# Low parts of the last layer's prepared weights by ScalarE and an adding transfer in place of a VectorE subtraction

## The chip, the cores and the metric

The kernel runs on one core of one Trainium2 chip. The metric is the device time of one execution in microseconds (us). The engines are called as the profile calls them: PE (TensorE), DVE (VectorE), ACT (ScalarE), POOL (GpSimd) and SP (SyncE, which here only begins transfers).

## The reference, cut to what matters

```python
def reference(**kwargs):
    ...
    attn_out = _attn_ref(**attn_kwargs)            # q, k, v, s: 2 x 8 heads, 576 rows, 64 wide
    x = np.ascontiguousarray(attn_out.transpose(0, 2, 1, 3)).reshape(B * S, H * D)   # 1152 x 512
    x = _moe_ref(x=x, **moe_kwargs)                # 8 experts, 512 -> 1024 -> 512, all of them for every row
    return _moe2_ref(x=x, **moe2_kwargs)

def _moe2_ref(x, w_in, w_out):                     # the last layer: 512 -> 2048 -> 512
    h = x @ w_in
    g = np.maximum(h, 0.0) + np.log1p(np.exp(-np.abs(h)))
    return (g @ w_out).astype(np.float32)
```

`w_in` and `w_out` are drawn as 64-bit floats, and the host hands them over as raw 64-bit words.

## The kernel before, in words

After attention, the rows (1152 x 512) stay in SBUF and the kernel walks 20 blocks `x` of 512 hidden columns: 16 for the experts (`NX`), then 4 for the last layer (`NL`). Products are made in fp32r. Each fp32 operand is split in a high part (rounded to fp32r by an ACT copy) and a low part (the raw word less the high part, on DVE or POOL), and each product is three matmuls: high by high, high by low, low by high. A block's first product is a seven-product scheme on 2 x 2 sub-blocks (class `Unit`, `p1` to `p7`, two units `a` and `b`, tile `ph`), its second is `downs` (tile `py`, three matmuls each, two PSUM banks `y1` and `y2`; `total`, line 554 or 378, adds a finished bank to `acc` on DVE).

The order is written out by hand, and each engine takes its instructions in the order in which the program writes them. `play` walks strings of tokens: `a1` ... `b7` are products of six matmuls, `d` is one step of `downs`, tokens with `=` or `w` start the preparation of the next block's weights. A block of an expert is one `A_SEQ` (30 steps) and one `B_SEQ` (34 steps):

```python
A_SEQ = "a1 b1 a2 b2 =0 d d a6 d d b6 d d a7 d d b7 =1 d a5 d b5 d a3 d b3 d a4 d b4 d d"
B_SEQ = ("d d =2 a1 d d b1 d a2 d b2 d a6 d b6 d a7 d b7 d a5 d b5 d d w0 a3 d d w2 b3 d d w1 a4 d d w3 b4")
```

After each step, `step` (line 1244) runs one piece of each list of side work. From block 2 to block 13 it also advances the generator `conv`, made by `convert` (line 1082), by one piece at every second step; what `conv` has not done by block 14 is done at once there. `convert` prepares the weights of the last layer, in 16 jobs of 4 blocks each:

- `fetch` (line 1099, SP) loads 128 x 512 64-bit words into the tile `f`, two of them per job.
- `narrow` (lines 1104 to 1125, six pieces) makes fp32 of them: DVE lines 1108, 1110, 1112, 1115, 1118, 1119, 1121, ACT line 1109, and one addition on POOL, line 1124. The result stands in the tile `c8` (128 x 8 x 256, one buffer; the trace calls it `c`).
- POOL (line 1140) adds and subtracts blocks, which gives all eight blocks of `c8`.
- For four pairs `c` of these blocks, ACT writes the high part to `ch` (line 1148), DVE writes raw less high to `cl` (line 1150), and SP stores both to the DRAM tiles `wd` (line 1154). `ch` and `cl` have three buffers each; a piece ends after line 1148 and after line 1150.

A job has 22 pieces (2 x 6, 2, 4 x 2). `c8` has one buffer, so line 1109 of the next job, which writes into it, comes after the last read of the old one. On SP the loads of the experts' raw weights (line 141, tile `raw`) and the fetches stand in one queue with these stores. On POOL the same queue has the sums of the experts' first weights (lines 161 to 170) and half of the low parts of their second weights (line 220). ACT copies finished products out of PSUM (lines 468 and 427) in the same queue as lines 1109 and 1148; in a unit, the copy after `a5` must be done before `a3` writes the same bank.

Of the kernel before, what the change touches and what calls it, by code (L numbers as in the profile page):

```python
# [13 lines left out]
AF = mybir.ActivationFunctionType  # L14
ALU = mybir.AluOpType
# [5 lines left out]
def attention_moe_ffn(ctx, tc, q, k, v, s, w_gate, w1, w2, w_in, w_out, out):  # L21
    nc = tc.nc
# [11 lines left out]
    NX = w1.shape[0]  # L34
# [18 lines left out]
    def f(ap):  # L53
        return ap.bitcast(F32)
# [506 lines left out]
    with tc.manual_schedule():  # L561
        with ExitStack() as att:
# [64 lines left out]
            for j, queue, engine in ((0, nc.sync, nc.gpsimd), (1, nc.scalar, nc.vector)):  # L627
                queue.dma_start(out=s0[j * D:j * D + NR, :],
                                in_=s.rearrange("b (x two) s -> two (b x) s", two=2)[j].unsqueeze(1).to_broadcast([B * NP, 4, S]))
# [452 lines left out]
        def convert(cv):  # L1082
            CW = WQ // 2
            top = float(np.uint32(0x47EFFFFF).view(np.float32))
            low = float(np.uint32(0x38100000).view(np.float32))
            half = 2.0 ** -20
            jobs = []
            for x in range(NL):
                for p in range(2):
                    jobs.append((1, x, p, [w_in[2 * x + p][:, c * CW:(c + 1) * CW] for c in range(2)]))  # L1090
                for r in range(2):
                    jobs.append((2, x, r, [w_out[2 * x + i][:, r * CW:(r + 1) * CW] for i in range(2)]))
            todo = [z for *_, c in jobs for z in c]
            got = {}

            def fetch(i):
                if i < len(todo):
                    t = cv.tile([P, 2 * CW], U32, tag="f64", name="f64")
                    nc.sync.dma_start(out=t, in_=todo[i].bitcast(U32))
                    got[i] = t  # L1100

            def narrow(i, m):
                t64 = got.pop(i)
                r = t64.rearrange("p (f two) -> p f two", two=2)
                lo, hi = r[:, :, 0], r[:, :, 1]
                t = cv.tile([P, CW], U32, tag="ct", name="ct")
                hf = hi.bitcast(F32)
                nc.vector.tensor_scalar(hf, hf, -top, top, ALU.max, ALU.min)
                nc.scalar.activation(out=m, in_=hf, func=AF.Abs)
                nc.vector.tensor_scalar(t, hi, 5, 2, ALU.logical_shift_left, ALU.logical_shift_right)  # L1110
                yield
                nc.vector.scalar_tensor_tensor(out=t, in0=hi, scalar=0xC0000000, in1=t,
                                               op0=ALU.bitwise_and, op1=ALU.bitwise_or)
                yield
                nc.vector.scalar_tensor_tensor(out=m, in0=m, scalar=low, in1=f(t), op0=ALU.is_ge, op1=ALU.mult)
                yield

                nc.vector.tensor_scalar(t, m.bitcast(U32), 0xFF800000, None, ALU.bitwise_and)
                nc.vector.tensor_scalar(lo, lo, 9, 0x35800000, ALU.logical_shift_right, ALU.bitwise_or)
                yield  # L1120
                nc.vector.scalar_tensor_tensor(out=f(t), in0=lo.bitcast(F32), scalar=half, in1=f(t),  # L1121
                                               op0=ALU.subtract, op1=ALU.mult)
                yield
                nc.gpsimd.tensor_tensor(out=m, in0=m, in1=f(t), op=ALU.add)  # L1124
                fetch(i + 2)
                yield

            fetch(0)
            fetch(1)
            for _ in range(4):  # L1130
                yield
            for j, (which, x, n, _) in enumerate(jobs):
                t = cv.tile([P, 8, HW], F32, tag="c8", name="c8", bufs=1)
                for c in range(2):
                    yield from narrow(2 * j + c, t[:, 2 * c:2 * c + 2, :].rearrange("p b n -> p (b n)"))
                for o, a, b, op in (((4, 0, 3, ALU.add), (6, 1, 0, ALU.subtract), (7, 4, 1, ALU.subtract),
                                     (5, 2, 7, ALU.subtract)) if which == 1 else
                                    ((4, 1, 0, ALU.subtract), (6, 3, 1, ALU.subtract), (5, 3, 4, ALU.subtract),
                                     (7, 2, 5, ALU.subtract))):
                    nc.gpsimd.tensor_tensor(out=t[:, o], in0=t[:, a], in1=t[:, b], op=op)  # L1140
                    if o == 6:
                        yield
                yield
                for c in range(4):
                    o = int(which == 1 and c == 0)
                    u = slice(2 * c + o, 2 * c + 2)
                    h, l = (cv.tile([P, 2, HW], F32R, tag="c" + k, name="c" + k, bufs=3)[:, o:] for k in "hl")
                    nc.scalar.activation(out=h, in_=t[:, u], func=AF.Copy)
                    yield
                    nc.vector.tensor_tensor(out=l, in0=t[:, u], in1=f(h), op=ALU.subtract)  # L1150
                    yield
                    for k, y in enumerate((h, l)):
                        d = wd[1][x, n][:, k, u] if which == 1 else wd[2][x][:, k, u, n]
                        nc.sync.dma_start(out=d, in_=f(y))
# [86 lines left out]
        tick = [0, 0, 0, 0]  # L1241
        dense = [False]

        def step(z=""):

            tick[0] += 1
            tick[1] += 1
            tick[2] = 0 if z[1:] == "2" else tick[2] + 1
            if x < XE:
                if tick[1] >= (5 if tick[3] > 10 and tick[3] % 2 else 3) and tick[2] > 2 and not dense[0]:  # L1250
                    next(gates, None)
                    tick[1] = 0
                    tick[3] += 1
            elif x < NX - 2 and tick[0] % 2:
                next(conv, None)
            for todo in (back, side, bot):
                while todo and next(todo[0], 1):
                    todo.pop(0)
# [15 lines left out]
        def play(seq, todo, d=None):  # L1274


            for z in seq.split():
                if z[0] in "=w":
                    dense[0] = z[0] == "w"
                if z[0] == "=":  # L1280
                    back.append(prep1(x + 1, int(z[1])))
                    continue
                if z[0] in "tu":
                    side.append(turn(int(z[1]), z[0] == "t"))
                    continue
                if z[0] == "w":
                    back.append(prep2(x + 1, int(z[1])))
                    continue
                if z[0] in "xy":
                    bot.append(prep_b(x + 1, z[1:]) if z[0] == "x" else prep_t(x + 1, int(z[1])))  # L1290
                    continue
                if z[0] in "EF":
                    side.append(h_steps(x, int(z[1]), z[0]))
                    continue
                if z[0] == "X":
                    bot.append(prep_b(x, z[1:]))
                    continue
                if z == "n":
                    flush()
                elif z == "d":  # L1300
                    next(d)
                else:
                    todo[z]()
                step(z)
# [19 lines left out]
        x = -1  # L1324
# [4 lines left out]
        for x in range(NH):  # L1329
# [44 lines left out]
            if x == XE - 1:  # L1374
                for _ in gates:
                    pass
                gt.close()
                conv = convert(cv.enter_context(tc.tile_pool(name="cv", bufs=2, reuse_waits="tile")))
# [56 lines left out]
```

## Time and profile before

| | us |
|---|---|
| median of three runs | 1071.31 |
| lowest and highest of them | 1070.62, 1071.97 |
| the profiled execution, as timed | 1070.41 |
| its span, first to last instruction | 1068.6 |

The busy share of an engine is an average over stages. The stage that matters here is the one in which `conv` runs: the first instruction of line 1109 starts 224.8 us into the span, and the last of line 1150 at 749.4 us. The views that follow cut the span there. A wait in the profile is named by the instruction that waited and by the one whose end released it. Matmuls overlap one another, so a busy PE is read from the distance between their starts as well.

### The profile page before, as it was taken

How to read it: one execution, taken by the hardware profiler on the slowest of the kernel's cores; microseconds unless marked ns; L12 is line 12 of the kernel's file. 1: busy time of each engine (PE TensorE's matmuls, PEld its weight loads, DVE VectorE, ACT ScalarE, POOL GpSimd, SP SyncE). 2: the span in 40 equal slices, each digit the busy share in tenths (PEclk: the TensorE clock that was granted, in tenths of full speed). 3: DMA queues.
4: the chain of work that ended last, by engine and by line, in shares of the span. 5: the costliest groups of instructions: out<-in, count | busy, mean ns of one | idle time of the engine just before them, and what ended most of it. 6: DMA issues, size and time to landing. Idle time of an engine off the chain costs nothing.

```text
span 1068.6 us, 18560 instructions
## 1 busy us (share of the span) xinstructions
PE 1053.4 (99%) x6804; PEld 937.4 (88%) x6804; DVE 767.9 (72%) x1701; ACT 512.5 (48%) x1216; POOL 341.0 (32%) x397
## 2 busy tenths in 40 slices
PE   7999999999999999999999999999999999999998
PEld 4777888898898888888898889889888889899997
DVE  5576566777889887898878888788545466377766
ACT  7999544344444444444444444444343356253432
POOL 8885303053543235261443434254120011000000
PEclk9999999999999999999999999999999999999999
DMA  6221111124443444434453433443220215464542
GB/s 198 83 80 55 41 40 40 40 99 128 149 139 119 157 143 134 141 106 129 149 167 125 142 129 129 146 141 98 67 73 1 79 60 159 158 195 154 165 138 90
DMA packets 74675, 122.53 MB, mean 115 GB/s; under 512 B 9056, under 2 KB 44896, under 8 KB 74584
## 3 DMA queue, kind: packets, MB, share of 16 engines
q1 hardware_dynamic: 74400, 121.13, 35.0%
q8 instruction: 54, 0.88, 0.3%
q14 instruction: 37, 0.30, 0.1%
q10 hardware_dynamic: 184, 0.20, 0.1%
HBM read 86.97 MB, written 33.82 MB: 113 GB/s over the span
## 4 chain that ended last, share of the span: by engine, by line
PE 90%; DVE 5%; ACT 2%; issue 1%; POOL 1%; DMA 1%; SPq 0%; POOLq 0%; ACTq 0%; DVEq 0%
PE ph L460 39%; PE py L536 38%; PE py L378 5%; PE sc L752 2%; PE pv L859 1%; PE tr L833 1%; POOL eb L815 1%; PE sc L756 1%; DVE acc L554 1%; PE pv L869 0%; ACT eb L802 0%; DVE w2l L220 0%; PE tr L827 0%; PE pg L1040 0%; PE tr L839 0%
## 5 line engine op out<-in xcount | busy, mean ns | idle before, releaser
L460 PE MATMUL ph<-xh,w1h 128*128 128x288 f32 x1120 | 331.7, 296 | 0.4 <-ACT v L468 0.3
L460 PE MATMUL ph<-xh,w1l 128*128 128x288 f32 x1120 | 330.9, 295 | 0.0
L460 PE MATMUL ph<-xl,w1h 128*128 128x288 f32 x1120 | 329.3, 294 | 0.0
L536 PE MATMUL py<-w2h,hh 128*128 128x512 f32 x620 | 246.4, 397 | 0.7 <-DVE acc L554 0.7
L536 PE MATMUL py<-w2h,hl 128*128 128x512 f32 x620 | 245.2, 395 | 0.0
L536 PE MATMUL py<-w2l,hh 128*128 128x512 f32 x620 | 245.0, 395 | 0.0
L460 PEld LDWEIGHTS ph<-xh,w1h 128*128 128x128 f32 x1120 | 210.0, 188 | 20.1 <-ACT v L468 1.5
L460 PEld LDWEIGHTS ph<-xl,w1h 128*128 128x128 f32 x1120 | 210.4, 188 | 18.0
L460 PEld LDWEIGHTS ph<-xh,w1l 128*128 128x128 f32 x1120 | 210.2, 188 | 0.0
L427 ACT ACTIVATE hh<-ph 128x288 fp32r<-128x288 f32 x192 | 78.6, 410 | 164.2 <-DVE ph L510 95.7
L468 ACT ACTIVATE v<-ph 128x288 f32<-128x288 f32 x160 | 64.5, 410 | 185.7 <-PE ph L460 183.5
L536 PEld LDWEIGHTS py<-w2h,hl 128*128 128x128 f32 x620 | 116.5, 188 | 28.4 <-DVE hl L434 0.3
L554 DVE SCALAR_TENSOR_TENSOR acc<-py,gate,acc 128x512 f32<-128x512 f32 x126 | 93.7, 744 | 49.6 <-PE py L536 49.6
L536 PEld LDWEIGHTS py<-w2h,hh 128*128 128x128 f32 x620 | 116.4, 188 | 11.2 <-DVE acc L554 1.1
L536 PEld LDWEIGHTS py<-w2l,hh 128*128 128x128 f32 x620 | 116.6, 188 | 9.5
L220 POOL TENSOR_TENSOR w2l<-raw,w2h 128x512 fp32r<-128x512 f32 x32 | 44.3, 1384 | 215.3 <-ACT w2h L218 215.3
L1124 POOL TENSOR_TENSOR c<-c,ct 128x512 f32<-128x512 f32 x32 | 43.3, 1354 | 217.5 <-DVE ct L1121 198.9
L434 DVE SCALAR_TENSOR_TENSOR hl<-ph,hh 128x288 fp32r<-128x288 f32 x192 | 86.4, 452 | 28.4 <-ACT hh L427 26.7
L155 DVE TENSOR_TENSOR w1l<-raw,w1h 128x512 fp32r<-128x512 f32 (+1 forms) x128 | 89.3, 698 | 7.5 <-ACT w1h L152 7.4
L499 DVE TENSOR_TENSOR t<-ph,v 128x288 f32<-128x288 f32 x80 | 36.3, 454 | 63.1 <-ACT v L468 62.3
L152 ACT ACTIVATE w1h<-raw 128x512 fp32r<-128x512 f32 (+1 forms) x128 | 73.1, 571 | 1.6 <-POOL raw L168 1.6
L468 ACT ACTIVATE u<-ph 128x288 f32<-128x288 f32 x80 | 32.6, 410 | 48.2 <-PE ph L460 46.7
(234 smaller groups left out, 1615.1 us busy)
## 6 DMA issues: line engine op xcount, KB each, us to landing
raw<-in_w SPq DMA_DIRECT2D x64, 512.0 KB
wd<-ch SPq DMA_DIRECT2D x56, 256.0 KB
wd<-cl SPq DMA_DIRECT2D x56, 256.0 KB
f<-in_w_in SPq DMA_DIRECT2D x16, 512.0 KB
f<-in_w_out SPq DMA_DIRECT2D x16, 512.0 KB
w1h<-wd SPq DMA_DIRECT2D x24, 256.0 KB
w1l<-wd SPq DMA_DIRECT2D x24, 256.0 KB
w2h<-wd SPq DMA_DIRECT2D x16, 256.0 KB
```

The source lines that it names most:

```text
L152: nc.scalar.activation(out=hi[:, o], in_=t[:, src], func=AF.Copy)
L155: nc.vector.tensor_tensor(out=lo[:, o], in0=t[:, src], in1=f(hi[:, o]), op=ALU.subtract)
L220: (nc.gpsimd if i else nc.vector).tensor_tensor(out=lo, in0=t[:, r], in1=f(hi), op=ALU.subtract)
L378: nc.tensor.matmul(o, u, v, start=(start and c == 0 and n == 0), stop=(c == 1 and n == 2), skip_group_check=True)
L427: nc.scalar.activation(out=hh, in_=z, func=AF.Relu)
L434: nc.vector.scalar_tensor_tensor(out=hl, in0=z, scalar=0.0, in1=f(hh), op0=ALU.max, op1=ALU.subtract)
L460: nc.tensor.matmul(o, u, v, start=(start and c == 0 and n == 0), stop=(c == 1 and n == 2), skip_group_check=True)
L468: nc.scalar.activation(out=t, in_=self.a, func=AF.Copy)
L499: defer(0, lambda: nc.vector.tensor_tensor(out=t, in0=self.c, in1=u4, op=ALU.add))
L536: nc.tensor.matmul(py[t], u, v, start=(k == 0 and n == 0), stop=(k == NF - 1 and n == 2))
L554: nc.vector.scalar_tensor_tensor(out=a, in0=py, scalar=gate_t[0][:, t, e:e + 1], in1=a, op0=ALU.mult, op1=ALU.add)
L1124: nc.gpsimd.tensor_tensor(out=m, in0=m, in1=f(t), op=ALU.add)
```

## The change

```diff
                     nc.scalar.activation(out=h, in_=t[:, u], func=AF.Copy)
                     yield
-                    nc.vector.tensor_tensor(out=l, in0=t[:, u], in1=f(h), op=ALU.subtract)
+                    nc.scalar.activation(out=l, in_=f(h), func=AF.Copy, scale=-1.0)
+                    nc.gpsimd.dma_start(out=f(l), in_=t[:, u], accum_op=ALU.add)
                     yield
+                    if c == 3:
+                        yield
+                        yield
+                        yield
                     for k, y in enumerate((h, l)):
                         d = wd[1][x, n][:, k, u] if which == 1 else wd[2][x][:, k, u, n]
                         nc.sync.dma_start(out=d, in_=f(y))
...
-            elif x < NX - 2 and tick[0] % 2:
+            elif x < NX - 2 and tick[0] * 8 % 15 < 8:
                 next(conv, None)
```

The subtraction on DVE goes. ACT writes minus the high part into `l` (line 1150 of the changed kernel), and a transfer that POOL begins (line 1151) reads the raw words from `c8` and adds them to `l` where it stands in SBUF. A job gets three empty pieces after its fourth pair (25 pieces in place of 22), and `conv` advances at 8 of 15 steps in place of 1 of 2. The stores are at line 1159 of the changed kernel.

How instructions move on ACT, in the queue around the end of a job. Before, this is the end of the third job; the number behind a tile's name tells buffers apart, `c_3814` is the old `c8` and `c_4167` the new one:

```order
L1148 ACTIVATE ch<-c_3814 128x512 [waits DMAHW1_49,Pool_49]
L468 ACTIVATE u<-ph 128x288 [waits PE_49]
L1148 ACTIVATE ch<-c_3814 128x512 [waits DMAHW0_49,Activation_49,Pool_49]
L152 ACTIVATE w1h_4136<-raw_3861 128x512 [waits DMAHW3_49]
L468 ACTIVATE u<-ph 128x288 [waits PE_49]
L152 ACTIVATE w1h_4155<-raw_3915 128x512 [waits DMAHW5_49]
L1109 ACTIVATE c_4167<-f_3896 128x512 [waits DMAHW4_49,DVE_49,Activation_49]
```

With the change, the same place (`c_3855` is the old tile, `c_4234` the new one):

```order
L1148 ACTIVATE ch<-c_3855 128x512 [waits DMAHW1_49,Pool_49]
L152 ACTIVATE w1h_4165<-raw_3915 128x512 [waits DMAHW4_49]
L1150 ACTIVATE cl<-ch 128x512 [waits DMAHW2_49,DMASW0_49,Activation_49]
L468 ACTIVATE v<-ph 128x288 [waits PE_49]
L152 ACTIVATE w1h_4214<-raw_3865 128x512 [waits Pool_49]
L427 ACTIVATE hh<-t_4208 128x288 [waits DVE_49]
L468 ACTIVATE v<-ph 128x288 [waits PE_49]
L1109 ACTIVATE c_4234<-f_3936 128x512 [waits DMASW3_49,DMASW2_49,DMAHW5_49,DMASW1_49,DVE_49]
```

ACT has a second instruction per pair, and line 1109 of the next job waits for the adding transfers of the old job (`DMASW`), where it waited for DVE.

On POOL, before, the end of one job's sums and the start of the next job (old tile `c_4508`, new tile `c_4858`):

```order
L1140 TENSOR_TENSOR c_4508<-c_4508 128x256
L1140 TENSOR_TENSOR c_4508<-c_4508 128x256 [waits Pool_49]
L1124 TENSOR_TENSOR c_4858<-c_4858,ct 128x512 [waits DVE_49,Activation_49,Pool_49]
L1124 TENSOR_TENSOR c_4858<-c_4858,ct 128x512 [waits DVE_49]
L220 TENSOR_TENSOR w2l<-raw_4574,w2h 128x512 [waits DMAHW6_49,PE_49,Activation_49]
```

With the change (old tile `c_4609`, new tile `c_4973`):

```order
L1140 TENSOR_TENSOR c_4609<-c_4609 128x256
L1140 TENSOR_TENSOR c_4609<-c_4609 128x256 [waits Pool_49] x2
L1151 DMA cl<-c_4609 128x256 [waits DMAHW0_49,Activation_49]
L1151 DMA cl<-c_4609 128x512 [waits DMAHW2_49,Activation_49]
L1151 DMA cl<-c_4609 128x512 [waits DMAHW6_49,Activation_49,Pool_49]
L1151 DMA cl<-c_4609 128x512 [waits DMAHW2_49,DMASW0_49,Activation_49]
L220 TENSOR_TENSOR w2l<-raw_4578,w2h 128x512 [waits DMAHW4_49,PE_49,Activation_49]
L1124 TENSOR_TENSOR c_4973<-c_4973,ct 128x512 [waits DMASW2_49,DMASW3_49,DMASW1_49,DVE_49]
L220 TENSOR_TENSOR w2l<-raw_4578,w2h 128x512 [waits Activation_49]
```

Four transfers per job now stand in POOL's queue, each waiting for ACT, ahead of the experts' low parts (line 220) and the next job's addition.

## Rows read from the trace of the kernel before

**Rows 1.** The page's first part: busy time of each engine over the span.
```profile
PE 1053.4 (99%) x6804; PEld 937.4 (88%) x6804; DVE 767.9 (72%) x1701; ACT 512.5 (48%) x1216; POOL 341.0 (32%) x397
```
**Rows 2.** Windows view: length, busy us (and instructions) per engine, clock, DMA share, GB/s.
```profile
224.00:750.00 526.00, 525.15 (x3046) 469.07 (x3045) 436.57 (x805) 238.21 (x538) 213.74 (x214) 1.00 0.41 134
...
750.00:865.00 115.00, 115.00 (x670) 102.68 (x669) 56.09 (x109) 41.51 (x93) 13.98 (x16) 1.00 0.19 59
```
**Rows 3.** Waits of PE from 224 to 750 us: us in total, times, longest.
```profile
PE py L536 <- DVE acc L554: 0.7, 2, 0.5
```
**Rows 4.** Timeline of PE at the longer of these waits: start, us, what.
```profile
373.79 0.29 PE L460 MATMUL ph<-xl,w1h 128*128 128x288 f32 x1
373.92 0.29 PE L460 MATMUL ph<-xh,w1l 128*128 128x288 f32 x1
374.68 0.50 PE L536 MATMUL py<-w2h,hh 128*128 128x512 f32 x1 [0.47 <-DVE acc L554]
```
**Rows 5.** Timeline of DVE ahead of that wait.
```profile
367.96 0.82 DVE L1108 TENSOR_SCALAR f<-f 128x512 f32<-128x512 f32 x1
368.81 0.85 DVE L1110 TENSOR_SCALAR ct<-f 128x512 uint32<-128x512 uint32 x1
...
369.95 0.86 DVE L1112 SCALAR_TENSOR_TENSOR ct<-f,ct 128x512 uint32<-128x512 uint32 x1
370.92 1.04 DVE L1115 SCALAR_TENSOR_TENSOR c<-c,ct 128x512 f32<-128x512 f32 x1
...
372.67 0.68 DVE L155 TENSOR_TENSOR w1l<-raw,w1h 128x512 fp32r<-128x512 f32 x1
373.27 0.69 DVE L1121 SCALAR_TENSOR_TENSOR ct<-f,ct 128x512 f32<-128x512 f32 x1
373.88 0.74 DVE L554 SCALAR_TENSOR_TENSOR acc<-py,gate,acc 128x512 f32<-128x512 f32 x1
```
**Rows 6.** Instructions on the tile `c`: ns min/median/max, first and last start in us.
```profile
L1148 ACT ACTIVATE ch<-c x64: 408/623/642, 247.1 to 748.8; 128x512 fp32r<-128x512 f32 x56, 128x256 fp32r<-128x256 f32 x8
L1150 DVE TENSOR_TENSOR cl<-c,ch x64: 415/684/1264, 248.7 to 749.4; 128x512 fp32r<-128x512 f32 x56, 128x256 fp32r<-128x256 f32 x8
L1109 ACT ACTIVATE c<-f x32: 663/680/699, 224.8 to 727.5; 128x512 f32<-128x512 f32 x32
```
**Rows 7.** Groups by line, 245 to 750 us: busy us, mean ns, idle before.
```profile
L1150 DVE TENSOR_TENSOR cl<-c,ch 128x512 fp32r<-128x512 f32 (+1 forms) x64 | 46.7, 729 | 2.3 <-ACT ch L1148 2.0
...
L468 ACT ACTIVATE v<-ph 128x288 f32<-128x288 f32 x85 | 34.2, 410 | 88.4 <-PE ph L460 86.8
```
**Rows 8.** Timeline of SP: one store, alone between quiet stretches.
```profile
378.77 0.33 SPq L1154 DMA_DIRECT2D wd<-ch  x1
382.80 0.33 SPq L1154 DMA_DIRECT2D wd<-cl  x1
```
**Rows 9.** Windows view around that store.
```profile
378.75:379.25 0.50, 0.50 (x6) 0.50 (x5) 0.50 (x2) 0.00 (x0) 0.50 (x1) 1.00 0.00 0
379.25:379.75 0.50, 0.50 (x5) 0.41 (x4) 0.50 (x2) 0.35 (x1) 0.42 (x2) 1.00 0.27 94
379.75:380.25 0.50, 0.50 (x5) 0.46 (x4) 0.50 (x2) 0.50 (x3) 0.50 (x1) 1.00 0.50 168
380.25:380.75 0.50, 0.50 (x6) 0.50 (x5) 0.50 (x1) 0.41 (x1) 0.50 (x2) 1.00 0.00 0
```
**Rows 10.** Windows view where two raw loads (from 363.73) and a fetch crowd.
```profile
364.50:365.50 1.00, 1.00 (x8) 0.91 (x7) 1.00 (x4) 0.00 (x0) 0.00 (x0) 1.00 0.69 184
...
368.50:369.50 1.00, 1.00 (x8) 0.91 (x7) 0.97 (x2) 0.69 (x2) 0.93 (x2) 1.00 0.73 287
369.50:370.50 1.00, 1.00 (x7) 0.86 (x6) 1.00 (x3) 1.00 (x4) 0.92 (x2) 1.00 0.00 0
```
**Rows 11.** Instructions on the tile `raw`, 224 to 750 us: the same columns as rows 6.
```profile
L220 DVE TENSOR_TENSOR w2l<-raw,w2h x22: 680/692/1734, 262.4 to 742.8; 128x512 fp32r<-128x512 f32 x22
L220 POOL TENSOR_TENSOR w2l<-raw,w2h x22: 1287/1298/1739, 263.6 to 743.5; 128x512 fp32r<-128x512 f32 x22
L161 POOL TENSOR_TENSOR raw<-raw x22: 734/956/1290, 269.6 to 746.8; 128x256 f32<-128x256 f32 x22
```
**Rows 12.** Timeline of DVE: the longest instruction of line 1108.
```profile
464.76 1.37 DVE L1108 TENSOR_SCALAR f<-f 128x512 f32<-128x512 f32 x1
```

## The prediction

> **What bounds the kernel now.** I read the busy times first: PE works 99% of the span, DVE 72%, ACT 48%, POOL 32% [rows 1]. A change that only moves work off DVE can therefore save no more than PE's idle time in the stage where that work stands. So I cut out the stage in which the last layer's weights are prepared. From 224 to 750 us PE is busy 525.15 of 526 us, at the full clock, while DVE has 436.57, ACT 238.21 and POOL 213.74 us of work [rows 2]. PE's idle time is 0.85 us. The view of waits names 0.7 of it, two waits of `downs` for the accumulation on DVE (line 554), and nothing else [rows 3].
>
> That figure is modelled, so I checked the longer wait in the order of time. The last matmul of one product starts at 373.92 and the next matmul at 374.68, where the neighbours stand 0.13 us apart [rows 4]. That is 0.63 us lost, where the view says 0.47. Taking 0.63 / 0.47 as a factor on 0.85 gives 1.1 us; I allow 1.7 us, twice the modelled figure, as the most that this stage can give back. What fills DVE ahead of that wait is the narrowing (lines 1108 to 1121) and the experts' low parts (line 155); no subtraction of line 1150 is among these rows [rows 5].
>
> **Removed.** 64 subtractions on DVE, 46.7 us with the times they lose to others [rows 7]. DVE's load falls from 436.57 to some 390 of 526 us (83% to 74%). None of it is on PE's path except through the backlog that makes PE wait, and the one I followed is built by other lines. After line 1150 goes, the accumulation at 373.88 is still behind the same narrowing rows. So I credit half of the idle time, 0.4 us, and keep 0 and 1.7 as the ends.
>
> **Moved.** The narrowing comes at 8 of 15 steps where it came at 1 of 2, so each of its runs is 6.7% denser on DVE. The first and the last of the 32 rows of line 1109 start at 224.8 and 727.5 us [rows 6]; between them lie 15 jobs of 22 pieces and 6 pieces, 336 pieces, so one piece is 1.496 us, a step of the order 0.748 us, and a piece of the changed kernel 0.748 x 15 / 8 = 1.40 us. The whole takes 4 + 16 x 25 = 404 pieces, 567 us. It starts a few pieces before 224.8, so its last store comes near 786 us in place of 750. Blocks 2 to 13 have 12 x 64 = 768 steps, or 409 pieces, so nothing is left to be done at once in block 14. From 750 to 865 us DVE has 56.09 of 115 us of work and DMA a share of 0.19 [rows 2]. The overhang costs nothing there.
>
> **Added on ACT.** 64 copies with a negative sign. The nearest row is the high part's copy of the same shape, 623 ns [rows 6]: 64 x 0.6 = 38 us, which lifts ACT from 238 to some 277 us of work, 45% to 50% over the longer stage. A single one delays the next eviction by up to 0.62 us. The tightest eviction I find is the copy after `a5`: three steps, `d b5 d`, lie between its product and `a3`, 3 x 0.748 = 2.2 us. The copy itself takes 0.41 us [rows 7], so ACT can be 1.8 us late there before PE stops. Two copies in a row (1.25 us) fit. Cost 0.
>
> **Added on POOL and the DMA engines.** 64 transfers of up to 256 KB. No row of before shows POOL beginning a transfer, nor one that adds. What matters is the time from ACT's copy to the landing.
> - Beginning it: at least what SP needs, 0.33 us [rows 8]. At most I take POOL's longest row, 1.74 us, behind another of 1.74 and a sum of 1.29 [rows 11], 4.8 us in all.
> - Moving it: an isolated store of the same size is begun at 378.77 and its packets are over by 380.25 [rows 8, 9], 1.5 us. Adding also reads what it overwrites; and beside others it takes longer: two raw loads and a fetch begun from 363.73 keep the DMA engines busy until about 369.5 [rows 10], so 5.0 us is the upper end.
> - With the copy (0.62): 2.45 us at least, 10.4 us at most. I take 4 us, the lower end plus a read more and half a POOL row, since the DMA share in this stage is 0.41 and POOL is busy 41% of the time [rows 2].
>
> Who waits for it? The stores of `l` on SP, some 2 to 3 us longer than now, with raw loads and fetches behind them; those are wanted half a block later (a block is 64 x 0.748 = 48 us). `cl` has three buffers, so line 1150 of a later pair comes at least 6 pieces, 8.4 us, after the one whose store must be done: 4 us and 1.5 us for the store fit. And line 1109 of the next job, on ACT, needs `c8` free. From the fourth pair's transfer to it there are 4 pieces, 4 x 1.40 = 5.6 us: 4 us fit here too. POOL's own time: 64 x 0.33 = 21 us at least, 64 x 1.74 = 111 us at most, onto 213.74 of 526 us. At most that makes 62%, with the experts' sums still ahead of their use. I set 0.1 us for all of it.
>
> **The sum.** 1070.41 - 0.4 + 0.1 = 1070.1 us for the profiled execution. The median is 0.90 us above that execution, so I predict **1071.0 us**. A measurement of this kernel can tell about 0.2% (2.1 us) from no change.
>
> **The rivals.**
> - *The transfer comes too late and ACT stands (slower).* If copy, begin and landing take more than 5.6 us, ACT waits at line 1109 with the evictions behind it; PE loses once ACT is 1.8 us late, so this decides from 7.4 us on. At the upper end, 10.4 us, ACT is 4.8 us late and PE loses up to 3.0 us where a tight eviction follows at once. There are 15 such job ends, and I count a tight spot soon after a third of them: 15 x 3.0 / 3 = 15 us, about 1086; at 8.7 us it is 15 x 1.3 / 3 = 6.5 us, 1077.5. For it: three queues are chained, and fetches of 512 KB crowd there. Against it: the isolated store, and ACT's slack. Chance 0.13.
> - *DVE's load does not fall (slower or the same).* POOL and DVE hold each other up: line 220 on DVE takes 0.68 us at best and 1.73 at worst [rows 11]. If each of 64 transfers holds DVE for about 0.7 us, the 46.7 us are given back, the backlogs stay, and denser runs add a few waits like that at 374: five times 0.5 us, 1073.8. Chance 0.06.
> - *All of PE's idle time goes (faster).* 1071.31 - 1.7 = 1069.6. Even that is 0.16%. To pass 0.2%, waits would have to go that no view shows. Chance of passing 0.2%: 0.04.
>
> One rule of the Trainium skill speaks against the change. Line 1108 on DVE, a tensor_scalar, takes up to 1.37 us beside work on POOL [rows 12], so the two engines do hold each other up in this kernel. The Trainium skill (SBUF — State Buffer, "SBUF: two separate sides") says that a transfer begun by GpSimd needs its descriptors written by GpSimd itself, and that VectorE's two-port modes shut it out until the instruction ends, so that it should be begun by another engine. No trace of before shows such a transfer; by that rule each transfer would be held for one such instruction, at most 1.37 us here, which makes my 4 us into 5.4 and leaves 0.2 of the 5.6 us: the first rival's side, with a few ends of a job late by less than the 1.8 us that PE allows. I gave the first rival 0.13, and not 0.10, for rows 12 alone.
>
> **How the numbers follow.** The forecast, a difference within 0.2%, has 0.77: its own range is 1069.6 to 1073. Slower by over 0.2% has 0.13 from the first rival, 0.04 from the second, 0.02 for costs not listed, together 0.19. Faster by over 0.2% has 0.04. Eight times in ten the time lies between 1069.4 and 1074.5 us: the low end is all idle time gone and the spread of the runs, the high end takes in the second rival and the mild part of the first.
>
> **What would show it.** In the profile after, line 1150 stands on ACT with about 0.62 us, 64 times, and is gone from DVE; DVE's load between 224 and 786 us is about 45 us less; the last store comes near 786. PE's idle time in that stage is between 0 and 2 us, and what it waits for is still line 554. Wrong would be: waits of ACT at line 1109 for a transfer with PE waiting for lines 468 or 427 after them, POOL rows for the transfers of over 2 us, or a PE idle time of more than 3 us.

## The result and the profile after

| | before | changed |
|---|---|---|
| median, us | 1071.03 | 1080.47 |
| profiled execution, us | 1070.41 | 1079.91 |
| its span, us | 1068.6 | 1077.6 |

The ratio is 1.0086, 95% interval 1.0072 to 1.0100: 9.4 us slower. The prediction was 1071.0 us, no difference.

The windows view of the changed kernel (length, busy us and instructions of PE, weight loads, DVE, ACT and POOL, clock, DMA share, GB/s), which answers to [rows 2]:

```profile
224.00:800.00 576.00, 568.72 (x3283) 505.16 (x3282) 419.22 (x781) 284.67 (x636) 265.75 (x284) 1.00 0.54 153
```

Before, PE stood 0.85 us between 224 and 750 us and not at all up to 865. Now it stands 576.00 - 568.72 = 7.28 us up to 800, with the clock at its upper level throughout. Since the ends of matmuls are modelled, this is somewhat less than the time lost. DVE is busy 419.22 of 576 us; nothing is short of throughput. So PE waits for something that is late, and the view of waits names it (engine, line waited for: us in total, times, longest). First PE, which answers to [rows 3]:

```profile
PE py L536 <- DVE acc L554: 3.8, 5, 0.9
PE ph L460 <- ACT v L468: 2.0, 1, 2.0
PE py L536 <- ACT hh L427: 1.2, 2, 0.8
```

Then ACT, from 224 to 800 us:

```profile
ACT cl L1150 <- DMA wd<-cl: 14.1, 10, 3.3
ACT c L1109 <- DMA cl<-c: 9.0, 4, 5.6
...
ACT c L1109 <- DMA wd<-cl: 3.2, 1, 3.2
```

These three rows make 26.3 us in which ACT stands for transfers, where it stood 1.2 before. It does so at two places: line 1150, where the oldest of three buffers of `cl` is not stored yet (14.1 us), and line 1109, where the single `c8` is still being read by the adding transfers (9.0 us; the 3.2 us at the same line are put down to a store). How that reaches PE is seen best in the chain of waits between 459 and 480 us (start, us, what):

```profile
458.89 0.63 ACT cl L1150
...
459.92 6.01 DMA cl<-c
...
465.94 4.44 DMA wd<-cl
...
470.49 0.64 ACT cl L1150
...
471.53 6.35 DMA cl<-c
...
478.06 0.66 ACT c L1109
478.72 0.31 ACT v L468
```

One adding transfer takes 6.01 us, the store that follows it 4.44; ACT's copy three pairs later has waited 3.30 us for that store; its own transfer takes 6.35 us, and line 1109 of the next job waits for it. ACT would have come to line 1109 at 472.46, 5.60 us before it started at 478.06: the late copy had left only 2.0 us between itself and line 1109. Behind line 1109 stands the eviction of line 468, and PE pays (timeline of PE, the two matmuls that waited):

```profile
473.08 0.50 PE L536 MATMUL py<-w2h,hh 128*128 128x512 f32 x1 [0.88 <-DVE acc L554]
...
479.07 0.40 PE L460 MATMUL ph<-xh,w1h 128*128 128x288 f32 x1 [2.03 <-ACT v L468]
```

The first of the two is the same lateness by another way: DVE's accumulation stood behind a low part of line 155, and that behind an ACT copy queued after line 1150.

The instructions on `cl` (ns min/median/max, first and last start) and the landing times of its transfers:

```profile
L1150 ACT ACTIVATE cl<-ch x64: 402/625/645, 247.0 to 787.1; 128x512 fp32r<-128x512 f32 x56, 128x256 fp32r<-128x256 f32 x8
L1151 POOL DMA_DIRECT2D cl<-c x64: 834/858/1217, 247.8 to 788.3; - x64
...
DMA to landing us min/median/max: 2.6/4.2/6.6
```

POOL needs 0.86 us to begin one, and it lands 2.6 to 6.6 us after its begin; the eight transfers of 128 KB make the low end, and no transfer of 256 KB lands in less than 3.2 us. Both ends can be looked at. Alone or nearly so, with SP beginning nothing between 507.52 and 512.01 us, a transfer of 256 KB begun at 509.24 moves its packets within 1.5 us (timeline of POOL, then the windows view, then its time to landing):

```profile
509.24 0.87 POOL L1151 DMA_DIRECT2D cl<-c  x1 [4.62 <-PE ph L460]
```

```profile
510.50:511.00 0.50, 0.50 (x6) 0.50 (x5) 0.50 (x1) 0.00 (x0) 0.50 (x1) 1.00 0.74 129
511.00:511.50 0.50, 0.50 (x6) 0.50 (x5) 0.50 (x1) 0.00 (x0) 0.42 (x1) 1.00 1.13 197
511.50:512.00 0.50, 0.50 (x6) 0.50 (x5) 0.50 (x2) 0.00 (x0) 0.00 (x0) 1.00 1.13 197
```

```profile
DMA to landing us min/median/max: 3.2/3.2/3.2
```

The one begun at 471.53 finds the DMA engines full of what SP began since 465.94, a raw load of 512 KB and six stores:

```profile
471.50:472.50 1.00, 0.70 (x6) 0.46 (x4) 0.83 (x2) 0.96 (x3) 0.92 (x2) 1.00 1.09 376
472.50:473.50 1.00, 0.42 (x2) 0.38 (x3) 1.00 (x2) 0.00 (x0) 0.92 (x2) 1.00 1.10 378
473.50:474.50 1.00, 1.00 (x8) 0.91 (x7) 1.00 (x3) 0.00 (x0) 1.00 (x2) 1.00 1.11 377
474.50:475.50 1.00, 1.00 (x7) 0.86 (x6) 0.90 (x2) 0.00 (x0) 0.92 (x2) 1.00 1.18 238
475.50:476.50 1.00, 1.00 (x9) 0.95 (x8) 0.97 (x2) 0.00 (x0) 0.40 (x1) 1.00 0.30 58
476.50:477.50 1.00, 0.54 (x3) 0.10 (x1) 0.41 (x1) 0.00 (x0) 0.00 (x0) 1.00 0.07 12
```

That transfers begun by different engines share the same DMA engines is also what the Trainium skill says (DMA: Bandwidth & Descriptors, "Issuing engines are not separate DMA queues"). The two transfers agree: the same 256 KB need 3.2 us from begin to landing alone and 6.35 us among SP's. The last 1.4 us before the landing at 477.88 are no crowd: from 476.50 on the DMA share is 0.07, about one of the 16 engines (0.07 x 16 = 1.1).

The crowd has a cause that the prediction saw only as a delay. The store of `cl` stands in SP's queue until the adding transfer has landed, and what is behind it stands too (waits of SP, then its timeline):

```profile
SPq L1159 <- DMA cl<-c: 167.7, 58, 7.7
```

```profile
460.54 0.43 SPq L1159 DMA_DIRECT2D wd<-ch  x1
465.94 0.38 SPq L1159 DMA_DIRECT2D wd<-cl  x1
466.42 0.42 SPq L141 DMA_DIRECT2D raw<-in_w  x1
```

SP begins nothing for 5 us and then, when the transfer has landed, seven in 5.1 us (465.94 to 471.04); the transfer begun at 471.53 comes behind them. One late landing so prepares the next. That is read from this one place; no run tests it alone.

### The profile page after: what moved, and what is told of

Its sections match the earlier page's. It is cut to its first block, busy times and chain, and to the rows that moved or that the text cites. A ratio compares the mean times of both kernels' runs of the same rounds, so it can differ in the third digit from the quotient of the medians.

```text
span 1077.6 us, 18756 instructions
## 1 busy us (share of the span) xinstructions
PE 1055.8 (98%) x6804; PEld 936.7 (87%) x6804; DVE 729.4 (68%) x1637; ACT 543.7 (50%) x1280; POOL 388.4 (36%) x461
## 4 chain that ended last, share of the span: by engine, by line
PE 73%; DVE 10%; DMA 7%; ACT 4%; POOL 3%; issue 3%; SPq 0%; DVEq 0%; ACTq 0%; POOLq 0%
PE ph L460 32%; PE py L536 30%; PE py L378 5%; DMA cl<-c 4%; DMA wd<-cl 1%; DVE hl L434 1%; PE sc L752 1%; PE pv L859 1%; DVE acc L554 1%; POOL c L1140 1%; PE tr L833 1%; DVE w1l L155 1%; DVE ct L1121 1%; DVE c L1115 1%; POOL eb L815 1%
## 5 line engine op out<-in xcount | busy, mean ns | idle before, releaser
L1151 POOL DMA_DIRECT2D cl<-c x64 | 55.6, 875 | 79.3 <-ACT cl L1150 35.2
```

The lines of the kernel that those rows point to most:

```text
L1151: nc.gpsimd.dma_start(out=f(l), in_=t[:, u], accum_op=ALU.add)
```

## The experiments

Three theories stood against one another. A: lateness, ACT stands behind transfers through two buffers. B: load, the transfers on POOL and the DMA engines and the copies on ACT slow all others. C: pace, the denser pieces make DVE's backlogs longer. Each ratio is to the kernel before on the same chip. PE idle is 576 less PE's busy time from 224 to 800 us (0.85 before; time at the lower clock counts as busy); the last two columns are ACT's waits for `DMA cl<-c` at line 1109 and for `DMA wd<-cl` at the copy to `cl`.

| run | median us | ratio (95%) | PE idle us | at 1109 | at the copy |
|---|---|---|---|---|---|
| changed | 1080.47 | 1.0086 (1.0072 to 1.0100) | 7.28 | 9.0 | 14.1 |
| e1 four low parts | 1078.66 | 1.0075 (1.0054 to 1.0095) | 6.82 | 24.1 | 0 |
| e2 raw words in two tiles | 1073.34 | 1.0021 (1.0011 to 1.0030) | 1.67 | 0 | 11.5 |
| e3 both | 1072.18 | 1.0008 (0.9998 to 1.0017) | 0.77 | 0 | 0 |
| e4 pace alone, 8 of 15 | 1071.56 | 1.0005 (0.9995 to 1.0015) | 0.61 | none | none |
| e5 no transfer | 1070.76 | 0.9998 (0.9988 to 1.0007) | 0.61 | none | none |
| e7 six empty pieces, 3 of 5 | 1078.36 | 1.0069 (1.0055 to 1.0082) | 5.83 | 2.3 | 16.1 |
| e8 no empty piece, 1 of 2 | 1108.06 | 1.0346 (1.0332 to 1.0360) | 25.08 | 64.1 | 1.4 |
| e9 as e3, no empty piece, 1 of 2 | 1074.16 | 1.0032 (1.0019 to 1.0044) | 2.29 | 1.4 | 0 |
| e10 as e7, four low parts | 1076.27 | 1.0054 (1.0039 to 1.0069) | 4.65 | 0.9 | 0 |
| e11 pace alone, 3 of 5 | 1077.58 | 1.0064 (1.0049 to 1.0079) | 6.01 | none | none |
| e12 no stores of high parts | 1073.51 | 1.0020 (1.0010 to 1.0030) | 1.58 | 13.9 | 7.4 |
| e13 as e9, no transfer | 1070.75 | 0.9998 (0.9989 to 1.0007) | 0.80 | none | none |

### The two buffers (e1, e2, e3)

```diff
-  cv.tile([P, 2, HW], F32R, tag="c" + k, ..., bufs=3)
+  cv.tile([P, 2, HW], F32R, tag="c" + k, ..., bufs=3 + (k == "l"))
```

> The changed kernel with four buffers of the low part in place of three, so that ACT's negative copy never waits for the store of the pair three before. Theory A (ACT stands behind late transfers, through two buffers: the low part's ring, 14.1 us of waits, and the single tile of raw words, some 12 us; PE loses where an eviction stands behind): ACT's waits for stores at the negative copy go from 14.1 us to under 1, part of the loss of 9 us comes back, about 1076 us. Theory B (the load itself, of transfers on POOL and the DMA engines and of copies on ACT, slows all others): no change, 1080 us. Theory C (the pace of 8 in 15 and the new places of the pieces make DVE's backlogs longer): 1080 us.

Measured: 1078.66 us, not to be told from the changed kernel. The wait at line 1150 is gone, and that at line 1109 grew from 9.0 to 24.1 us:

```profile
ACT c L1109 <- DMA cl<-c: 24.1, 8, 8.1
```

The wait moved to the next buffer in the chain. The time alone speaks against theory A, which had 1076 us where B and C had 1080; the waits speak for it, but not for its sum of two halves.

```diff
-  t = cv.tile([P, 8, HW], F32, tag="c8", name="c8", bufs=1)
+  ts = [cv.tile([P, 4, HW], F32, tag="c8" + z, name="c8" + z, bufs=1) for z in "ab"]
...
```

> The changed kernel with the tile of raw words as two tiles of four blocks, so that the next job's first ACT instruction waits only for the transfers of the job's first two pairs, which began some 6 pieces earlier. Theory A: ACT's waits for transfers at that instruction go from some 12 us to under 2, part of the loss comes back, about 1076 us. Theories B and C: 1080 us.

Measured: 1073.34 us, more than expected came back. ACT's 11.5 us at the ring remain and cost PE little: they are 11 waits of at most 3.3 us, and none is followed by a wait at line 1109.

Both edits together:

> Both: four buffers of the low part and two tiles of raw words. Theory A: nothing on ACT waits for a transfer any more, 1071 to 1073 us. Theory B: 1079 us or more, with PE's idle time as in the changed kernel. Theory C: 1079 us.

Measured: 1072.18 us, not told apart from before. All 64 transfers, all 64 copies and the new pace are still there, so at this pace theories B and C explain at most 1.7 parts in a thousand.

### Pace and copies alone (e4, e5)

```diff
-  nc.scalar.activation(out=l, in_=f(h), func=AF.Copy, scale=-1.0)
-  nc.gpsimd.dma_start(out=f(l), in_=t[:, u], accum_op=ALU.add)
+  nc.vector.tensor_tensor(out=l, in0=t[:, u], in1=f(h), op=ALU.subtract)
```

> The kernel before, with only the three empty pieces per job and the pace of 8 in 15; the subtraction stays on DVE and no transfer is added. Theory A: 1071 to 1072 us. Theory B: 1071 to 1072 us. Theory C: 1075 us or more, with PE waiting for the accumulation on DVE about as often as in the changed kernel.

Measured: 1071.56 us, and PE idle 0.61 us. Theory C falls for the pace of 8 in 15.

```diff
   nc.scalar.activation(out=l, in_=f(h), func=AF.Copy, scale=-1.0)
-  nc.gpsimd.dma_start(out=f(l), in_=t[:, u], accum_op=ALU.add)
```

> The changed kernel without the adding transfer: ACT still writes the negative high part, and SP stores it as it is. It leaves out the addition of the raw word, so the last layer's low parts are wrong. Theory A (late transfers): no transfer, nothing to be late, 1070 to 1071.5 us, so ACT's 64 copies cost nothing and DVE's lighter load gives back at most 1 us. Theory B (load): if the copies on ACT are the load that hurts, 1075 us or more; if the transfers' are, 1071 us.

Measured: 1070.76 us, ratio 0.9998. This is the best case of the whole idea, DVE relieved at no cost in transfers, and it gives nothing that can be measured. At this pace no version of the change can be expected to beat the kernel before by more than the interval of this run allows, 0.12%.

### More and less time before the next job (e7, e8)

```diff
   if c == 3:
       yield
       yield
       yield
+      yield
+      yield
+      yield
...
-  elif x < NX - 2 and tick[0] * 8 % 15 < 8:
+  elif x < NX - 2 and tick[0] * 3 % 5 < 3:
```

> The changed kernel with six empty pieces after a job's fourth pair in place of three, at 3 of 5 steps so that all jobs still end before block 14. From the last transfer to the next job's first ACT instruction there are 7 pieces of 1.25 us, 8.7 us in place of 5.6, but 7.5 in place of 8.4 us for the ring of three low parts. Theory A: ACT's waits for transfers at that instruction fall from 9 us to under 3, its waits for stores at the negative copy grow past 14 us; since the split alone gave back 7 us and the fourth buffer 2, about 1075 us. Theory B: 1080 us or more, since the same load is squeezed into fewer steps.

Measured: 1078.36 us. The waits moved as expected, 2.3 us at line 1109 and 16.1 at the ring, but the time stayed 3.4 us above the expectation. e10 and e11 below tell why.

```diff
-  if c == 3:
-      yield
-      yield
-      yield
...
-  elif x < NX - 2 and tick[0] * 8 % 15 < 8:
+  elif x < NX - 2 and tick[0] % 2:
```

> The changed kernel with no empty pieces, at 1 of 2 steps as before the change: 1.5 us from the last transfer to the next job's first ACT instruction in place of 5.6. Theory A: every one of the 15 job ends now waits 3 to 4 us on ACT, 40 us or more of waits for transfers in all, and the time goes up to 1085 to 1110 us. Theory B: 1080 us, as the load is the same.

Measured: 1108.06 us, as theory A has it. The load is the same as in the changed kernel, the waits are not:

```profile
ACT c L1109 <- DMA cl<-c: 64.1, 13, 6.8
```

Against e9, which has the same pace and the same empty pieces (none), the two buffers are worth 34 us. With the buffers as in the change, the loss is 37 us without empty pieces at 1 of 2 steps, and 9 us with three of them at 8 of 15.

### The pace of 3 in 5 (e10, e11)

e7 with the fourth low part of e1:

> Six empty pieces per job at 3 of 5 steps (the run of 1078.4 us) and four buffers of the low part. Theory A, that lateness alone counts and only moved from one buffer to the other there: ACT's waits at the negative copy go from 16 us to under 1, those at the next job's first instruction stay near 2, and the time is 1071 to 1073 us. Theory C', that the denser pieces at 3 of 5 cost time by themselves: 1075 us or more though ACT waits for no transfer.

Measured: 1076.27 us with hardly a wait for an adding transfer. Theory A missed; something else costs some 5 us at this pace.

e4 with the six empty pieces and the pace of e7:

> The kernel before with six empty pieces per job at 3 of 5 steps; the subtraction stays on DVE, no transfer is added. Theory A: 1071 to 1072 us. Theory C': 1074 us or more, from DVE's backlogs of denser narrowing.

Measured: 1077.58 us without any transfer. So e7 was no clean test of theory A: the pace alone costs what e7 lost. The trace of e11 shows one large piece of it, at the very start of the stage (timeline of DVE, of PE, then the windows view):

```profile
228.33 0.43 DVE L1108 TENSOR_SCALAR f<-f 128x512 f32<-128x512 f32 x1 [4.63 <-DMA f<-in_w_in]
```

```profile
233.75 0.79 PE L536 MATMUL py<-w2h,hh 128*128 128x512 f32 x1 [2.80 <-DVE acc L554]
```

```profile
230.50:233.00 2.50, 0.45 (x4) 0.21 (x2) 2.46 (x5) 0.30 (x1) 2.14 (x3) 1.00 0.00 0
233.00:240.00 7.00, 6.25 (x20) 5.58 (x21) 5.93 (x10) 2.19 (x5) 4.81 (x5) 0.51 0.23 75
240.00:245.00 5.00, 5.00 (x31) 4.50 (x31) 4.90 (x11) 1.85 (x5) 0.00 (x0) 1.00 0.00 0
```

The first narrowing is reached before its fetch has landed, DVE stands 4.63 us with an accumulation queued behind, PE stands 2.80 us, and from 233 us on, near the end of that stand, PE's clock is granted at 0.51, the lower of its two levels (1.2 GHz), for 7 us.

A second piece stands in e10, where the clock stayed at its upper level (timeline of PE):

```profile
521.50 0.50 PE L536 MATMUL py<-w2h,hh 128*128 128x512 f32 x1 [1.71 <-DVE acc L554]
```

DVE works from 506.38 to 523.31 us there without a pause that the view shows, with two narrowings in that stretch, and the accumulation comes behind them; e4 has no stand of PE for DVE there. At the start of the stage e10 loses 1.68 us as e11 does, so these two stands are 3.39 of its 4.65 us. Both are theory C at the denser pace: DVE's backlog behind the narrowing. (ACT also waits for the stores of the high parts, 3.6 us in e10 and 6.1 in e11, where the empty pieces stand ahead of the fourth pair's stores in the program; no stand of PE was traced to these waits.)

### What the transfers' load costs (e9, e13)

e3 with the edit of e8:

> Four buffers of the low part and two tiles of raw words, with no empty pieces and at 1 of 2 steps as before the change. The next job's first ACT instruction stands 5 pieces, 7.5 us, behind the second pair's transfer. Theory A: no more than 3 us of waits for transfers on ACT, 1071 to 1073 us, and with DVE lighter than before perhaps 1070.5. Theory B: 1079 us.

Measured: 1074.16 us, though ACT waits only 1.4 us for adding transfers: theory A left 3 us open.

e9 with its transfer left out, as in e5:

> The run with both buffers and no empty pieces at 1 of 2 steps (1074.2 us), without the adding transfer: ACT writes minus the high part and SP stores that, so the addition is left out and the last layer's low parts are wrong. If the 3 us that stayed there are the transfers' own load (POOL beginning them while DVE narrows): 1070.5 to 1071.5 us. If they are ACT's 64 copies at these places: 1074 us as with the transfers.

Measured: 1070.75 us. So at the old pace the transfers' own load costs 1074.16 - 1070.75 = 3.4 us, and ACT's copies nothing: theory B is right there, for the transfers. Where it bites can be read from line 1108 on DVE. The groups by line have it at 726 ns in the mean in e9 and 538 in e13:

```profile
L1108 DVE TENSOR_SCALAR f<-f 128x512 f32<-128x512 f32 x32 | 23.2, 726 | 0.4 <-DMA f<-in_w_in 0.4
```

```profile
L1108 DVE TENSOR_SCALAR f<-f 128x512 f32<-128x512 f32 x32 | 17.2, 538 | 0.1
```

and the timelines of POOL and DVE in e9 show the longest case, 1.99 us beside a transfer's begin and the low part of line 220 on POOL:

```profile
456.56 0.87 POOL L1152 DMA_DIRECT2D cl<-c8b  x1 [2.08 <-issue]
457.13 1.62 POOL L220 TENSOR_TENSOR w2l<-raw,w2h 128x512 fp32r<-128x512 f32 x1
```

```profile
457.05 1.99 DVE L1108 TENSOR_SCALAR f<-f 128x512 f32<-128x512 f32 x1
```

In e13, without the transfer, the same low part came earlier and the same narrowing was not held:

```profile
454.64 1.29 POOL L220 TENSOR_TENSOR w2l<-raw,w2h 128x512 fp32r<-128x512 f32 x1 [10.89 <-ACT w2h L218]
```

```profile
456.20 0.42 DVE L1108 TENSOR_SCALAR f<-f 128x512 f32<-128x512 f32 x1
```

So the transfer's place in POOL's queue moved line 220 onto line 1108. DVE works without a pause after it, and PE stands in e9 at 464.18 us (0.77 us, behind the eviction of line 468) and at 472.48 (0.66 us, behind line 554), where e13 has no stand. These two are 1.43 of the 1.49 us by which the idle times of PE differ; the rest of the 3.4 us is not traced.

In the changed kernel line 1108 has 591 ns in the mean, against 572 before, so there this load is small.

### Less beside the transfers (e12)

```diff
...
   for k, y in enumerate((h, l)):
       d = ...
-      nc.sync.dma_start(out=d, in_=f(y))
+      if k:
+          nc.sync.dma_start(out=d, in_=f(y))
```

> The changed kernel without the stores of the high parts (16.8 MB less for the DMA engines beside the transfers); the last layer loads the low parts twice, so its products are wrong. If the transfers land late because they share the DMA engines with what SP has begun: the median from begin to landing falls from 4.2 us to 3.3 to 3.8, ACT's waits for transfers and stores (26 us in all) fall below half, and the time is 1073 to 1076 us. If they land late for a reason of their own: 4.2 us and 1080 us as now.

Measured: the median landing is 3.7 us, the time 1073.51 us, both within the range expected of shared DMA engines. The sum of waits is not: 13.9 and 7.4 us are more than half of 26.3. The longest is 4.6 us where it was 5.6. (The stores left out are 56 of 256 KB and 8 of 128 KB, 15.7 MB.) With 21 us of waits PE loses 1.58 us here, with 26 it lost 7.28: the sum of ACT's waits does not price them. That the length of the single stand does is a guess from these two runs.

## Why the prediction was wrong

**The bound** held. PE's idle time was the most that could be gained, and e5 and e13, ratio 0.9998 both, gained nothing clear of the noise; a credit of 0.4 us is too small to be seen in them. "The one I followed is built by other lines" was right: without line 1150 on DVE, PE still stands 0.61 us.

**The pace** costs nothing, as predicted: e4 is 0.05% above before, within its interval. That the last low part stands at 787 us, where the end was worked out as 786, is luck: in e4 and e5, which lose nothing, it stands at 778.6 and 777.0, so the working was some 8 us too long, and the 9 us lost made it up. **ACT's copies at cost 0** were right (0.625 us each, e5, e13). **Beginning a transfer** at 0.86 us lies inside its bounds and near the lower end; with POOL's queue ahead of it one took longer than the 4.8 us of the bound (copy at 421.27, begin at 426.69), and no wait of ACT or PE is put down to that one.

**The step that failed** is the moving: "I take 4 us, the lower end plus a read more and half a POOL row", and its use, "4 us fit here too". The 4 us were to hold copy, begin and landing. From begin to landing alone the median is 4.2 us and the longest 6.6; with the copy, the link from ACT's copy to the landing is 7.0 us at 458.89 and 7.4 us at 470.49, and even the transfer that met no crowd (copy at 507.97, landing 3.2 us after 509.24) took 4.5. No transfer of 256 KB in the trace took less than 4.2: my 4 us was under the best case. The lower end had come from a store's packets, over 1.5 us after its begin in [rows 8, 9]; no row of before shows a landing. I had the upper end, 5.0 us of moving, from [rows 10] (5.8 us if counted from the begin at 363.73, as the 1.5 us are), and let a value near the lower end decide against slacks of 5.6 and 8.4 us. A wait is made by the late ones, and there are 15 ends of jobs.

The ring was sized worse still: I set 1.5 us for the store, the isolated one of [rows 8, 9]; the one in the chain takes 4.44 us, and from the copy at 458.89 to that store's end at 470.38 pass 11.5 us, against 8.4 us. And I treated the two buffers as two independent checks, where the lateness of one starts the other late: the copy at 470.49 stood 3.30 us, and the slack of 5.6 us behind it was 2.0. SP's queue I priced as a delay that costs nothing, "wanted half a block later"; its stores now stand 167.7 us for landings, and what it begins afterwards in a bunch lies in front of the next transfer.

**The first rival** was what happened, by its mechanism and place: ACT at line 1109 with line 468 behind it, and PE late after a landing. Its price, 1077.5 to 1086 us, holds 1080.47, but in part by luck. It let PE lose from 7.4 us on, by a slack of 5.6 us and 1.8 us more; the transfer that cost PE 2.03 us did take 7.4 us, but with a slack of 2.0 us, and ACT was 5.60 us late. The rival knew nothing of the ring, which made that slack small. It counted five tight ends of jobs; ACT does wait at five of the fifteen (12.2 us with the 3.2), yet PE stands right behind only one of them, and 5.0 of the 7.0 us in the list of its waits come through the accumulation of line 554 and the copies of line 427. It had a chance of 0.13; the crowd of [rows 10] is a row that should have given it more.

**The second rival**, DVE and POOL holding each other up, is no part of the 9 us that can be seen (e3 is 0.08% above before), but costs 3.4 us at the old pace.

**The rule on descriptors** that I let raise the first rival by 0.03 shows little in the begins: 834, 858 and 1217 ns are the shortest, the median and the longest, so the longest is 0.36 us over the median. (The 1.37 us of [rows 12], from which I priced it, are not the longest row of line 1108 before: one at 561.84 took 1.52 us.) What the runs show is the other direction, a VectorE instruction held while GpSimd works. The Trainium skill has that too (SBUF — State Buffer, "Who interferes with whom": with VectorE in a two-port mode, whoever issues first gets the shared pair for the whole instruction, and the other is blocked). The 1.99 us of e9 agree in that line 1108 ends at 459.04, 0.29 us after line 220 on POOL; which of the two came first the starts, 457.05 and 457.13, do not settle.

What stays open: how much of the 9.4 us is line 1109 alone. e2, without that wait, brings back 7 of them, e1 shows the wait at the ring feeding it, and e3 at 1.0008 and e5 at 0.9998 are not told apart by their intervals. And of the 5 us that e10 loses, two stands of PE explain 3.4.

## What to carry to other kernels

When work moves from an engine to a transfer, do not ask whether an isolated transfer's packets fit the slack; ask whether the latest landing does, among what the other queues have begun, and follow each buffer that it holds to the in-order engine that will want it next. A wait that is removed at one buffer can turn up whole at the next (e1). And first ask what the relieved engine would give back at all: leaving the new work out (e5) answered that in one run, nothing.

## What the runs showed that was not expected

The same 64 transfers cost from nothing measurable (e3) to 37 us (e8), by buffers, empty pieces and pace alone. A stand of PE of 2.80 us was followed by 7 us at the lower clock in e11, so one late fetch cost more than the stand itself. The length of the stand alone does not tell: in the changed kernel the clock stayed at the upper level after one of 2.03 us, and in e7 it was granted at the lower level for 3.4 us after a stand of 2.02 us (ended at 233.15) and again after one of 1.84 us (ended at 522.72):

```profile
233.30:236.70 3.40, 3.40 (x11) 2.99 (x12) 3.37 (x6) 0.50 (x2) 1.66 (x2) 0.50 0.19 48
523.50:527.00 3.50, 3.50 (x14) 3.13 (x13) 1.76 (x4) 1.37 (x3) 3.50 (x4) 0.52 0.46 150
```

And a change of pace from 8 in 15 to 3 in 5, with three more empty pieces per job and nothing else (e4 to e11), cost 6.0 us.
